# Four edits to a fused linear-attention and SwiGLU kernel: the order of its opening, the split of a weight block, the place of the row sums, and the last chunk of the output

## The chip, the cores and the metric

The kernel runs on one core of one Trainium2 chip. The metric is the device time of one execution in microseconds (us), of which several are taken; medians are quoted. Profiles show one execution each, and their span is 1.8 to 2.2 us shorter than the time of the same execution. Times in a profile count from the start of its span. All runs here were in the fast state (granted TensorE clock 0.995 to 1.0; 0.979 to 0.981 in the run with merged stores). "PE" is TensorE, "DVE" VectorE, "ACT" ScalarE, "POOL" GpSimd, "SP" the engine whose queue issues most transfers.

## The reference

```python
# attention: B=8, H=8, S=576, D=64          FFN: 4608 rows, d_model=512, d_ff=1536
kv  = einsum('bhsd,bhse->bhde', k, v)
out = einsum('bhsd,bhde->bhse', q, kv)
x   = out / sqrt(mean(out*out, -1) + 1e-6) * g_norm        # per head, then heads side by side
xn  = x / sqrt(mean(x*x, -1) + 1e-6) * rms_g
y   = (silu(xn @ w_gate) * (xn @ w_val)) @ w_out           # float32
```

## The kernel before

The rows are done in nine batches: the first 512 rows of each of the eight sequences, then their last 64 rows together. For each batch PE does twelve "up" units (the gate and the val products of 128 of the 1536 columns) and four "down" chunks. The attention of batch n+1 is woven between the up units of batch n. Weights arrive as float32, and are scaled and cast to bf16 ("rounded") on ACT, DVE or POOL.

The loads of the opening all go through one queue, in this order: k, v and q of batch 0, the weight blocks, k of batch 1, a third of w_out, v and q of batch 1, the rest of w_out, batch 2. The weight blocks, and what batch 0 does with the third one (units 4 to 7):

```python
W_BLOCKS = [(0, 2), (2, 4), (4, 8), (8, 12)]          # in units of 128 columns

def load_w(blk, name, queue):
    j0, j1 = W_BLOCKS[blk]
    ...                                               # a staging tile, [128, NS, columns]
    queue.dma_start(out=ap, in_={"g": wg_view, "v": wv_view}[name][:, :, j0 * 128 : j1 * 128])
...
for s in range(2):
    round_w(2, "g", s, SC)                            # SC is ACT
    round_w(2, "v", s, DVE)
for i in range(2):
    ffn.gate_pair(i, 256, ffn.up_pair(i, 256))        # units 0..3, second half of the rows
    round_w(2, "g", 2 + i, SC)
    round_w(2, "v", 2 + i, DVE)
```

The first two units take their 512 rows in halves of 256 (A, then Z), whose attention runs just before. PE is kept busy by dummy products (`warm`) while it waits. The state of batch 0 goes out of PSUM in two copies of 64x64 for each pair of heads:

```python
def put_state0(j, ps):
    for u in range(2):
        rows = slice(u * D, u * D + D)
        DVE.tensor_copy(out=kv_all[rows, 0, j, rows], in_=ps[rows, rows])
```

At the end of batch 0, with the q of batch 1 cast by three instructions on DVE and one on ACT:

```python
for i in range(4):
    cast_q(1, slice(2 * i, 2 * i + 2), SC if i == 2 else DVE)
...
down_part(0, 0, 4); down_part(1, 0, 4)
att1.kv_products((0, 1, 2, 3)); att1.kv_copy()
down_part(2, 0, 4)
turns.q_turn(0, SC); turns.q_turn(1, DVE)             # PE turns q of batch 1
down_part(3, 0, 4)
round_wo(1, 0, 2, DVE)                                # second third of w_out
```

In the later batches, the place of the attention's steps by unit (`o` is the product, `sums` the row sums on DVE, `head`, `guess` and `root` the norm, `scale` and `x_rows` the scaled x and its transpose by DMA, issued on the SP queue):

```python
kv0, os = (2, (4, 5, 7, 8)) if n == 1 else (0, (2, 4, 6, 8))
for c, u in enumerate(os):
    steps[u].append(lambda a=a, c=c: a.o(c))
    steps[u + 1].append(lambda a=a, c=c: a.sums(c))
steps[10] += [a.head]
steps[11] += [a.guess, a.root]
for c in range(T):
    steps[11] += [lambda a=a, c=c: a.scale(c), lambda a=a, c=c: a.x_rows(c)]
```

The last batch stores each chunk, after one copy of 128x512 on ACT, by two transfers on the SP queue.

## Time and profile before

| | before |
|---|---|
| time, median of the first 3 runs | 327.01 us |
| span of the profile | 325.2 us |
| PE busy | 315.5 us, 97% |
| first product of the FFN | 17.9 us |
| end of batch 0's up units | 40.7 us |
| first product of batch 1 | 56.94 us |
| last product ends, then span ends | 320.75, 325.2 us |

PE is the engine to look at, and since it is busy at 97% the only thing to gain is the time in which it waits or runs dummies. The page of the kernel before, its first part (busy us, share of the span, instructions):

```profile
PE 315.5 (97%) x1908; PEld 156.4 (48%) x1908; DVE 181.7 (56%) x374; ACT 178.3 (55%) x314; POOL 16.8 (5%) x37
```

PE's waits in the kernel before (who waited for whom: total us, times, longest):

```profile
PE g_ps L471 <- DMA xnt<-xna: 0.8, 1, 0.8
PE v_ps L471 <- DVE wv_sb L203: 0.6, 1, 0.6
```

The first of these two lines is one hole in the middle, before batch 3; PE's waits list has nothing else after 57 us. The second, like the lines left out here, is of the opening. Here is the hole in the timeline of the kernel before (start, length, engine, instruction, and in brackets the idle time before it and what ended it):

```profile
112.83 10.52 PE L508 MATMUL o_ps<-wo_sb,h_sb 128*128 128x512 bf16 x48
115.75 2.50 DVE L377 TENSOR_TENSOR xna<-outa,s1y 128x512 bf16<-128x512 bf16 x4
116.53 6.26 SPq L384 DMA_TRANSPOSE xnt<-xna  x4
124.17 1.02 PE L471 MATMUL g_ps<-xnt,wg_sb 128*128 128x512 bf16 x4 [0.81 <-DMA xnt<-xna]
```

DVE starts to scale x 2.92 us after the down chunks begin (115.75 - 112.83); four transposes follow on SP, and the last lands too late. From the start of this down phase to batch 3 it is 11.34 us, where the next batches take 10.36: the hole with its restart costs 0.98 us.

Why the last one is late, the DMA view of the stretch from 115 to 122 us shows. Beside the packets of the transposes it has one packet of a queue that the profile labels "instruction" (queue: packets, MB, share of 16 engines):

```profile
q8 instruction: 1, 0.02, 1.2%
```

In the trace this is one packet of 16 KB, under way from 117.18 to 118.47 us. The first transpose, which overlaps it, takes 2.34 us to issue and lands after 3.48; the other three take 1.21 to 1.22 us and land after about 2.5.

The opening is bound by loads. The stretches of the kernel before (columns: stretch, its length, busy time and count of PE, weight loads, DVE, ACT, POOL, then granted clock, DMA share, GB/s):

```profile
18.00:20.00 2.00, 1.95 (x20) 1.50 (x18) 1.77 (x7) 1.44 (x4) 1.72 (x4) 1.00 1.05 381
20.00:22.00 2.00, 2.00 (x25) 1.82 (x23) 2.00 (x6) 1.94 (x3) 1.83 (x4) 1.00 1.05 389
22.00:24.00 2.00, 2.00 (x21) 1.81 (x19) 1.12 (x2) 1.24 (x2) 0.15 (x1) 1.00 1.03 382
```

The DMA share is 1.03 to 1.05 here, so the engines are not idle; that a transfer then lands when the bytes ahead of it have gone through is the author's estimate from this. The q of batch 1 shows what the landing means for PE (timeline before):

```profile
42.63 0.62 ACT L106 CAST qb<-st 128x512 bf16<-128x512 f32 x1 [0.86 <-DMA st<-in_q_dram]
42.70 1.09 DVE L108 CAST qb<-st 128x512 bf16<-128x512 f32 x3
44.66 1.06 PE L780 MATMUL att_ps<-identity,qb 128*128 128x128 bf16 x16
45.35 1.17 POOL L108 CAST wo_sb<-st 128x512 bf16<-128x512 f32 x2 [6.12 <-DMA st<-in_moe_w_out_dram]
46.37 0.70 DVE L108 CAST wo_sb<-st 128x1024 bf16<-128x1024 f32 x1
```

It lands at 42.6, is cast by 43.8, and PE turns it at 44.66: slack of 0.9 us. And the tail before, the last copy and the two stores behind it (timeline of all engines, then SP alone):

```profile
320.79 0.59 ACT L106 COPY o_sb<-o_ps 128x512 f32<-128x512 f32 x1 [2.00 <-PE o_ps L508]
```

```profile
321.40 1.11 SPq L521 DMA_DIRECT2D out_dram<-o_sb  x2
```

### The profile page before, as it was taken

To read this page: it belongs to the slowest core of one execution; us is meant where nothing else is said; L and a number is where in the kernel's file an instruction comes from. 1 tells how busy PE (TensorE), PEld (TensorE's weight loads), DVE (VectorE), ACT (ScalarE), POOL (GpSimd) and SP (SyncE) were. 2 spreads that over 40 slices of the span, in tenths; PEclk is the share of its full clock that TensorE was granted. 3 is DMA by queue.
4 is the path that set the end of the run, shared out by engine and by line. 5 is a ranking of instruction groups with operands and counts; after the bars stand their busy time and mean duration, and the time that the engine had idled before them with its cause. 6 is when DMAs were issued, how large, how long until landed. Compare 5 with 4: busy or idle time off the path is not lost.

```text
span 325.2 us, 5068 instructions
## 1 busy us (share of the span) xinstructions
PE 315.5 (97%) x1908; PEld 156.4 (48%) x1908; DVE 181.7 (56%) x374; ACT 178.3 (55%) x314; POOL 16.8 (5%) x37
## 2 busy tenths in 40 slices
PE   7899999999999998999999999999999999999994
PEld 3684455544454444444544454445544444444441
DVE  4876657569436852676167715780578057904310
ACT  3567357666756575557655755666554355233321
POOL 1251323000000000000000000000000000000000
PEclk9999999999999999999999999999999999999999
DMA  8999999794369626971696179956200640060014
GB/s 260 346 379 387 376 373 290 211 288 133 64 177 289 152 46 162 303 171 33 161 315 170 33 147 199 299 156 156 81 2 16 159 85 0 18 179 1 0 34 98
DMA packets 73861, 54.87 MB, mean 169 GB/s; under 512 B 42088, under 2 KB 65644, under 8 KB 73836
## 3 DMA queue, kind: packets, MB, share of 16 engines
q1 hardware_dynamic: 73536, 53.95, 59.1%
q10 hardware_dynamic: 300, 0.59, 0.5%
q8 instruction: 15, 0.25, 0.3%
q14 instruction: 10, 0.08, 0.1%
HBM read 37.75 MB, written 9.44 MB: 145 GB/s over the span
## 4 chain that ended last, share of the span: by engine, by line
PE 90%; DMA 5%; SPq 1%; DVE 1%; POOL 1%; issue 0%; ACT 0%
PE g_ps L471 28%; PE v_ps L471 27%; PE o_ps L508 26%; DMA st<-in_moe_w_val_dram 3%; PE att_ps L271 2%; DMA st<-in_q_dram 2%; PE att_ps L342 2%; PE v_ps L488 1%; SPq L384 1%; PE g_ps L508 1%; PE g_ps L488 1%; PE v_ps L508 1%; DMA xnt<-xna 1%; POOL wv_sb L203 1%; PE att_ps L337 0%; PE att_ps L284 0%
## 5 line engine op out<-in xcount | busy, mean ns | idle before, releaser
L477 DVE TENSOR_TENSOR h_sb<-silu,v_ps 128x512 bf16<-128x512 bf16 x104 | 71.2, 685 | 110.3 <-PE v_ps L471 81.4
L471 PE MATMUL v_ps<-xnt,wv_sb 128*128 128x512 bf16 x416 | 106.9, 379 | 0.8 <-DVE wv_sb L203 0.6
L471 PE MATMUL g_ps<-xnt,wg_sb 128*128 128x512 bf16 x416 | 106.8, 379 | 0.8 <-DMA xnt<-xna 0.8
L476 ACT ACTIVATE silu<-g_ps 128x512 bf16<-128x512 f32 x104 | 62.6, 602 | 67.1 <-PE g_ps L471 66.0
L508 PE MATMUL o_ps<-wo_sb,h_sb 128*128 128x512 bf16 x408 | 90.0, 379 | 0.0
L508 PEld LDWEIGHTS <-h_sb 128*128 128x128 bf16 x432 | 41.9, 98 | 49.3 <-issue 0.3
L471 PEld LDWEIGHTS <-wv_sb 128*128 128x128 bf16 x416 | 40.7, 98 | 50.3 <-DVE wv_sb L203 1.2
L471 PEld LDWEIGHTS <-wg_sb 128*128 128x128 bf16 x416 | 38.5, 98 | 41.2 <-issue 2.2
L106 ACT COPY o_sb<-o_ps 128x512 f32<-128x512 f32 x34 | 19.9, 587 | 39.3 <-PE o_ps L508 39.3
L360 DVE TENSOR_REDUCE ssq<-sq 128x16 f32<-128x1024 bf16 x28 | 34.2, 1220 | 1.0
L351 ACT ACTIVATE sq<-att_ps 128x512 bf16<-128x512 f32 x28 | 16.7, 597 | 14.0 <-PE att_ps L342 11.2
L106 ACT CAST vb<-st 128x512 bf16<-128x512 f32 (+2 forms) x35 | 20.1, 627 | 4.0 <-DMA st<-in_v_dram 3.9
L377 DVE TENSOR_TENSOR xna<-outa,s1y 128x512 bf16<-128x512 bf16 x28 | 17.5, 687 | 0.2
L353 ACT CAST outa<-att_ps 128x512 bf16<-128x512 f32 x28 | 16.2, 580 | 0.0
L106 ACT CAST qb<-st 128x1024 bf16<-128x1024 f32 (+1 forms) x15 | 14.2, 987 | 1.9 <-DMA st<-in_q_dram 1.9
L106 ACT CAST kb<-st 128x512 bf16<-128x512 f32 (+1 forms) x25 | 14.0, 619 | 0.0
L359 DVE TENSOR_TENSOR sq<-sq,gsq 128x512 bf16<-128x512 bf16 x28 | 11.7, 418 | 0.0
L342 PEld LDWEIGHTS <-qt 128*128 128x128 bf16 x96 | 7.4, 98 | 5.7
L342 PE MATMUL att_ps<-kv_all,qt 128*128 128x128 bf16 x96 | 9.3, 219 | 0.0
L271 PEld LDWEIGHTS <-kb 128*128 128x128 bf16 x120 | 7.7, 98 | 2.8
L583 PE MATMUL att_ps<-kv_all 128*128 128x256 bf16 (+1 forms) x34 | 7.6, 357 | 1.2 <-DVE sel L572 1.2
L271 PE MATMUL att_ps<-vb,kb 128*128 128x128 bf16 x120 | 8.7, 219 | 0.0
(123 smaller groups left out, 154.4 us busy)
## 6 DMA issues: line engine op xcount, KB each, us to landing
out_dram<-o_sb SPq DMA_DIRECT2D x16, 512.0 KB, 3.2
st<-in_q_dram SPq DMA_DIRECT2D x7, 1024.0 KB, 7.3
st<-in_k_dram SPq DMA_DIRECT2D x6, 1024.0 KB, 10.3
st<-in_v_dram SPq DMA_DIRECT2D x6, 1024.0 KB, 11.6
st<-in_moe_w_out_dram SPq DMA_DIRECT2D x3, 1024.0 KB, 13.4
st<-in_moe_w_gate_dram SPq DMA_DIRECT2D x2, 1024.0 KB, 12.3
st<-in_moe_w_val_dram SPq DMA_DIRECT2D x2, 1024.0 KB, 13.1
st<-in_k_dram SPq DMA_DIRECT2D x4, 288.0 KB, 4.9
```

The source lines that it names most:

```text
L106: engine.copy(out=dst, in_=src)
L271: PE.matmul(ps, lhsT=bufs[b]["k"][:, t, hs, :], rhs=bufs[b]["v"][:, t, hs, :], start=(first and t == 0), stop=(last and t == T),)
L342: PE.matmul(cols, lhsT=self.qt[:, j, 128 * c : 128 * c + 128], rhs=kv_all[:, self.n, j, :], start=(j == 0), stop=(j == NS - 1),)
L351: SC.activation(out=self.sq[c][:, 0], in_=ps, func=ACT.Square)
L353: SC.copy(out=self.outa[c], in_=ps)
L359: DVE.tensor_tensor(out=sq[:, 1], in0=sq[:, 0], in1=gsq8, op=OP.mult)
L360: DVE.reduce_sum(out=self.ssq[:, c], in_=sq, axis=AX.X)
L377: DVE.tensor_tensor(out=self.xna[c], in0=self.outa[c], in1=self.alpha[:, c, :].to_broadcast([128, H, D]), op=OP.mult)
L471: PE.matmul(ps, lhsT=wt[:, s, j * 128 : (j + 1) * 128], rhs=x[:, s, :], start=(s == 0), stop=(s == NS - 1),)
L476: SC.activation(out=silu, in_=g_ps, func=ACT.Silu)
L477: DVE.tensor_tensor(out=self.h[:, j, :], in0=silu, in1=v_ps, op=OP.mult)
L508: PE.matmul(self.o_ps[c], lhsT=self.h[:, j, c * 128 : (c + 1) * 128], rhs=wo_sb[:, j, :], start=(j == 0), stop=(j == NF - 1),)
```

## The change

Four edits in one. (1) The opening is reordered: one state copy of 128x128, casts of q moved off DVE's critical stretch (one to POOL), the first gate products in quarters, so that they can start after one turned chunk of x. (2) The third weight block is split in two, so that units 4 and 5 have their weights sooner, and POOL rounds half of each. (3) The sums, the head and the guess move up one unit. (4) The last chunk is computed in three column parts, copied by ACT, ACT and DVE, and stored in halves on two queues. The core of the diff:

```diff
-    W_BLOCKS = [(0, 2), (2, 4), (4, 8), (8, 12)]
+    W_BLOCKS = [(0, 2), (2, 4), (4, 6), (6, 8), (8, 12)]
...
     def put_state0(j, ps):
-        for u in range(2):
-            rows = slice(u * D, u * D + D)
-            DVE.tensor_copy(out=kv_all[rows, 0, j, rows], in_=ps[rows, rows])
+        DVE.tensor_copy(out=kv_all[:, 0, j, :], in_=ps[:, 0:128])
...
+    ffn = Ffn(0)
+    first = ffn.pair_banks()
+    for lo in (0, 128):
+        for u in range(2):
+            ffn.half_unit(first[0], u, wg_sb, u, lo, lo + 128)
     oZ = rows_of(Z)
+    for u in range(2):
+        ffn.half_unit(first[1], u, wv_sb, u, 0, 256)
...
-    for s in range(2):
-        round_w(2, "g", s, SC)
-        round_w(2, "v", s, DVE)
+    for s in range(NS):
+        round_w(2, "g", s, SC if s < 2 else GP)
+        round_w(2, "v", s, DVE if s < 2 else GP)
     for i in range(2):
-        ffn.gate_pair(i, 256, ffn.up_pair(i, 256))
-        round_w(2, "g", 2 + i, SC)
-        round_w(2, "v", 2 + i, DVE)
+        banks = [b.rearrange("p (u t) -> p u t", u=2) for b in rows_banks()] if i == 0 else None
+        ffn.gate_pair(i, 256, ffn.up_pair(i, 256, banks=banks))
     broadcast_gsq()
+    for s in range(NS):
+        round_w(3, "g", s, SC if s < 2 else GP)
+        round_w(3, "v", s, DVE if s < 2 else GP)
...
-            kv0, os = (2, (4, 5, 7, 8)) if n == 1 else (0, (2, 4, 6, 8))
+            kv0, os = (2, (4, 5, 7, 8)) if n == 1 else (0, (2, 4, 6, 7))
-            steps[10] += [a.head]
-            steps[11] += [a.guess, a.root]
+            late = int(n == 1)
+            steps[9 + late] += [a.head]
+            steps[10 + late] += [a.guess]
+            steps[11] += [a.root]
...
+        def down_last(self, c):
+            o_sb = osb_pool.tile([128, 2, d_model], FP32, name="o_sb")[:, 0, :]
+            parts = (
+                (0, 256, ops_pool, "o_ps", SC), (256, 384, gps_pool, "g_ps", SC), (384, 512, vps_pool, "v_ps", DVE),
+            )
+            for lo, hi, p, nm, engine in parts:
+                ...                                  # 12 products of hi - lo columns
+                cast(engine, o_sb[:, lo:hi], ps)
+                for d0, done in ((0, 256), (256, 512)):
+                    if hi == done:
+                        for u in range(2):
+                            r0 = (2 * c + u) * S + MAIN
+                            (nc.sync if u or hi < d_model else nc.scalar).dma_start(
+                                out=out[r0 : r0 + TAIL, d0:done], in_=o_sb[u * TAIL : (u + 1) * TAIL, d0:done]
+                            )
```

(Also in the diff: fewer and longer dummy products, the order of the casts and of the gate scale, the rounding of the fourth block under its new number.)

More of the change, by code (lines that the diff above doesn't have):

```diff
@@ L477, in up, with pair_banks, half_unit, up_pair @@
             DVE.tensor_tensor(out=self.h[:, j, :], in0=silu, in1=v_ps, op=OP.mult)
-        def up_pair(self, i, lo, between=()):
-            x = xnts[self.n]
-            g_ps = gps_pool.tile([128, 2, 256], FP32, name="g_ps")
-            v_ps = vps_pool.tile([128, 2, 256], FP32, name="v_ps")
-            for ps, wt in ((g_ps, wg_sb), (v_ps, wv_sb)):
-                for u in range(2):
-                    j = 2 * i + u
-                    for s in range(NS):
-                        PE.matmul(
-                            ps[:, u, :], lhsT=wt[:, s, j * 128 : (j + 1) * 128], rhs=x[:, s, lo : lo + 256],
-                            start=(s == 0), stop=(s == NS - 1),
-                        )
-                    for f in between[2 * (wt is wv_sb) + u :][:1]:
+        def pair_banks(self):
+            return (
+                gps_pool.tile([128, 2, 256], FP32, name="g_ps"),
+                vps_pool.tile([128, 2, 256], FP32, name="v_ps"),
+            )
+        def half_unit(self, ps, u, wt, j, lo, hi):
+            for s in range(NS):
+                PE.matmul(
+                    ps[:, u, lo % 256 : lo % 256 + hi - lo], lhsT=wt[:, s, j * 128 : (j + 1) * 128],
+                    rhs=xnts[self.n][:, s, lo:hi], start=(s == 0), stop=(s == NS - 1),
+                )
+        def up_pair(self, i, lo, between=(), banks=None):
+            banks = banks or self.pair_banks()
+            for k, wt in enumerate((wg_sb, wv_sb)):
+                for u in range(2):
+                    self.half_unit(banks[k], u, wt, 2 * i + u, lo, lo + 256)
+                    for f in between[2 * k + u :][:1]:
                         f()
-            return g_ps, v_ps
+            return banks
         def gate_pair(self, i, lo, banks):
@@ L534, in down @@
             self.down_out(c)
+        def down_last(self, c):
+            o_sb = osb_pool.tile([128, 2, d_model], FP32, name="o_sb")[:, 0, :]
+            parts = (
+                (0, 256, ops_pool, "o_ps", SC), (256, 384, gps_pool, "g_ps", SC), (384, 512, vps_pool, "v_ps", DVE),
+            )
+            for lo, hi, p, nm, engine in parts:
+                ps = p.tile([128, MAIN], FP32, name=nm)[:, 0 : hi - lo]
+                for j in range(NF):
+                    PE.matmul(
+                        ps, lhsT=self.h[:, j, c * 128 : (c + 1) * 128], rhs=wo_sb[:, j, lo:hi],
+                        start=(j == 0), stop=(j == NF - 1),
+                    )
+                cast(engine, o_sb[:, lo:hi], ps)
[5 more added lines that the diff above has]
+                                out=out[r0 : r0 + TAIL, d0:done], in_=o_sb[u * TAIL : (u + 1) * TAIL, d0:done]
+                            )
     DVE.memset(kv_all[:, B - 1], 0.0)
@@ L599, in turn_q0 @@
         bank = att_pool.tile([128, 512], FP32, name="att_ps")
-        warm(bank, dummies, 256)
+        warm(bank, dummies)
         ps = bank.bitcast(BF16).rearrange("p (j i t) -> p j i t", j=NS, i=2)
@@ L615, in state0 @@
         ps = att_pool.tile([128, 512], FP32, name="att_ps")
-        warm(ps, dummies, 256)
+        warm(ps, max(dummies, 1), 512 if dummies else 128)
         kv_pair(ps[:, 0:128], 0, j, True, True)
@@ L641, in x_turn, with rows_banks @@
         to_rows(x, cols.n, cols.lo // 128 + c, bank.bitcast(BF16)[:, 0:512].rearrange("p (j t) -> p j t", j=NS), engine)
+    def rows_banks():
+        return [ops_pool.tile([128, MAIN], FP32, name="o_ps") for _ in range(2)]
     def rows_of(cols):
-        banks = [ops_pool.tile([128, H, D], FP32, name="o_ps") for _ in range(2)]
+        banks = [b.rearrange("p (h d) -> p h d", h=H) for b in rows_banks()]
         for c in range(2):
@@ L657 @@
     kv0 = state0(0, 0)
-    kv1 = state0(1, 5)
+    kv1 = state0(1, 3)
     put_state0(0, kv0)
@@ L662 @@
     put_state0(1, kv1)
-    qps = turn_q0(0, 4)
+    qps = turn_q0(0, 2)
     cast_kv(0, "k", 2, DVE)
@@ L667 @@
     put_q0(0, qps, 1, SC)
-    kv2 = state0(2, 6)
-    cast_kv(0, "k", 3, DVE)
-    cast_kv(0, "v", 3, SC)
-    put_state0(2, kv2)
-    gam_ps = att_pool.tile([128, 8], FP32, name="att_ps")
+    gam_ps = att_pool.tile([128, 512], FP32, name="att_ps")
     PE.matmul(gam_ps[:, 0:5], lhsT=gam[0:5, :], rhs=ident32[0:5, 0:5], is_transpose=True, start=True, stop=True)
@@ L675 @@
     DVE.tensor_scalar(out=rowscale, in0=gam_ps[:, 0:NS], scalar1=gcol[:, 0:1], scalar2=None, op0=OP.mult)
-    DVE.scalar_tensor_tensor(
-        out=gsq, in0=gcol, scalar=1.0 / d_model, in1=gcol, op0=OP.mult, op1=OP.mult
-    )
-    for i in range(2):
-        DVE.tensor_copy(out=sel[i * D : (i + 1) * D, 1, i : i + 1], in_=gsq[i * D : (i + 1) * D, :])
+    kv2 = state0(2, 3)
+    cast_kv(0, "k", 3, DVE)
+    put_state0(2, kv2)
+    cast_kv(0, "v", 3, DVE)
     banksA = [gps_pool.tile([128, MAIN], FP32, name="g_ps"), vps_pool.tile([128, MAIN], FP32, name="v_ps")]
@@ L686 @@
     square(A, 2, banksA[1])
-    kv3 = state0(3, 2)
+    kv3 = state0(3, 1)
+    DVE.scalar_tensor_tensor(
+        out=gsq, in0=gcol, scalar=1.0 / d_model, in1=gcol, op0=OP.mult, op1=OP.mult
+    )
     put_state0(3, kv3)
-    cast_q0(1, hs0, DVE)
-    cast_q0(1, hs1, DVE)
+    for i in range(2):
+        DVE.tensor_copy(out=sel[i * D : (i + 1) * D, 1, i : i + 1], in_=gsq[i * D : (i + 1) * D, :])
     A.alloc_sums()
-    warm(A.bank, 4, 256)
+    warm(A.bank, 1)
     columns(A, 3, banksA[1])
     square(A, 3, banksA[1])
-    warm(A.bank, 3, 256)
+    warm(A.bank, 1)
     A.sums()
     oA = rows_of(A)
+    cast_q0(1, hs0, DVE)
+    cast_q0(1, hs1, GP)
+    A.head()
     qps = turn_q0(1, 0)
-    A.head()
     A.root_by_table(lambda: put_q0(1, qps, 0, DVE))
@@ L703 @@
         for s in range(NS):
-            round_w(0, name, s, GP)
+            if name == "g" or s < 2:
+                round_w(0, name, s, GP)
     banksZ = [gps_pool.tile([128, MAIN], FP32, name="g_ps"), vps_pool.tile([128, MAIN], FP32, name="v_ps")]
-    warm(banksZ[0], 4, 256)
+    warm(banksZ[0], 2)
     for j in range(NS):
@@ L710 @@
     squares(Z, 1, banksZ[1])
+    for s in (2, 3):
+        round_w(0, "v", s, SC)
     xs = [A.scale(c, oA[c]) for c in range(2)]
-    x_turn(A, 0, xs[0], DVE, 1)
+    x_turn(A, 0, xs[0], DVE)
     x_turn(A, 1, xs[1], DVE)
@@ L722 @@
     SC.preload_act_table(ACT.Silu)
-    ffn = Ffn(0)
     xs = [Z.scale(c, oZ[c]) for c in range(2)]
@@ L728 @@
     clear_tail_rows(0, GP)
-    halves = [ffn.up_pair(0, 0)]
     def turnsZ():
@@ L733, in turnsZ @@
         x_turn(Z, 1, xs[1], DVE)
-    halves.append(ffn.up_pair(1, 0, (lambda: None, turnsZ)))
-    ffn.gate_pair(0, 0, halves[0])
-    ffn.gate_pair(1, 0, halves[1])
-    for blk in (2, 3):
+    second = ffn.up_pair(1, 0, (lambda: None, turnsZ))
+    ffn.gate_pair(0, 0, first)
+    ffn.gate_pair(1, 0, second)
+    for blk in (2, 3, 4):
         for name in ("g", "v"):
@@ L756, in broadcast_gsq @@
         DVE.tensor_copy(out=gsq8, in_=ps[:, 0:D].unsqueeze(1).to_broadcast([128, H, D]))
-    for s in range(2):
-        round_w(2, "g", s, SC)
-        round_w(2, "v", s, DVE)
+    for s in range(NS):
+        round_w(2, "g", s, SC if s < 2 else GP)
+        round_w(2, "v", s, DVE if s < 2 else GP)
     for i in range(2):
-        ffn.gate_pair(i, 256, ffn.up_pair(i, 256))
-        round_w(2, "g", 2 + i, SC)
-        round_w(2, "v", 2 + i, DVE)
+        banks = [b.rearrange("p (u t) -> p u t", u=2) for b in rows_banks()] if i == 0 else None
+        ffn.gate_pair(i, 256, ffn.up_pair(i, 256, banks=banks))
     broadcast_gsq()
+    for s in range(NS):
+        round_w(3, "g", s, SC if s < 2 else GP)
+        round_w(3, "v", s, DVE if s < 2 else GP)
     alloc_q(1)
@@ L789 @@
     for s in (2, 3):
-        round_w(3, "v", s, GP)
+        round_w(4, "v", s, GP)
     for j in range(4, NF):
@@ L793 @@
         for s in {4: (0, 1), 5: (2,), 6: (3,)}.get(j, ()):
-            round_w(3, "g", s, SC)
+            round_w(4, "g", s, SC)
         if j == 6:
             for s in (0, 1):
-                round_w(3, "v", s, DVE)
+                round_w(4, "v", s, DVE)
         if j >= 8:
@@ L951 @@
                 ffn.up(unit)
+            elif n == B and unit == NF + T - 1:
+                ffn.down_last(unit - NF)
             else:
```

## The prediction

> **What bounds the kernel now.** TensorE. The page has PE busy 315.5 of 325.2 us at full clock. Three places are open. (1) The opening: the stretches view shows PE busy 2.91, 3.09, 3.67, 3.83 of 4 us from 4 to 20 us, partly dummy matmuls; the first FFN product starts at 17.9; batch 0's up phase ends at 40.7, though 12 units of 1.73 need 20.8. (2) A hole of 0.81 us at 123.3, before batch 3, on the DMA transpose of x; PE waits nowhere else after 57 us. (3) The tail: last matmul ends at 320.8, copy of 512 columns 0.59, two stores issued one after the other (321.4, 321.9), end 325.2.
>
> **The opening is also bound by loads.** The DMA rows show 345 to 390 GB/s from 4 to 52 us, and casts wait for landings: second block's val weights 25.4, third 31.0, output weights 36.6, q of batch 1 about 42.6, output weights 45.35 and 48.1. The change moves no byte ahead of batch 1's q, so these times should stay.
>
> **Opening.** State copies: two of 0.23 become one of about 0.25, four times. The q casts leave DVE's way; quarters let PE start after one turned chunk; v rounding is shared with ACT. First FFN product: 17.9 to about 16.8. The second pair's val weights still land about 20.1, so units 2-3 gain only 0.4. The split block removes most waits of units 4 and 5: the up phase ends about 39.2, 1.5 us early. Then batch 1's q at 42.6 plus three DVE casts (1.09) holds PE's q turn to about 43.8, against 44.66 before. **Of 1.5 us only about 0.85 survives**; the rest becomes a new PE wait of 0.5 to 1.3 us near 43.
>
> **Sums.** Before batch 3, DVE does unit 11's product, guess 0.9 and root 0.68, then scales from 115.75. Sums, head and guess move up a unit, but four units then carry 8.0 us of DVE work in about 7.1, so a backlog eats part: scales 0.65 earlier, hole 0.81 to 0.2. Gain 0.6.
>
> **Tail.** 128-column matmuls run at about 0.055 us each in the trace, so 12x256 + 24x128 cost as much as 12x512 (2.6). The last copy falls from 0.59 to about 0.28, and the last two stores start together on two queues, saving one issue (0.55). [...] Gain 0.85.
>
> **Sum:** 0.85 + 0.6 + 0.85 = 2.3: 327.0 to **324.7 us**, range 323.3 to 326.2 for 8 in 10. Faster by over 2%: 0.02; within 2%: 0.96; slower by over 2%: 0.02.
>
> **What would show it.** PE's waits: a new one on the DVE q cast of batch 1, the wv_sb wait gone; batch 1's first product near 56.1 (before 56.94); the wait before batch 3 below 0.4; other batches still 33.1 apart; the last copy on DVE near 0.28 and the end 3.3 to 3.6 us after the last matmul instead of 4.4.
>
> **What would make it wrong.** Loads landing at other times (earlier: up to 0.7 more is kept); POOL's rounding of half of the split blocks late against PE; DVE's backlog holding a PSUM bank, with new PE waits at units 9 to 11 in every batch; 128-column matmuls slower than thought.

## The result, and the profile after

The changed kernel took 325.53 us (325.46 to 325.61, 4 runs), the kernel before 326.68 us (326.2 to 327.15, 4 runs). The ratio is 0.9965, 95% interval 0.9947 to 0.9983. The gain is 1.15 us; 2.3 were predicted.

| us, from the profiles | before | after |
|---|---|---|
| first product of the FFN | 17.90 | 17.62 |
| end of batch 0's up units | 40.71 | 39.59 |
| q of batch 1 has landed | 42.63 | 43.22 |
| first product of batch 1 | 56.94 | 57.01 |
| start of batch 2's down chunks, to batch 3 | 11.34 | 10.36 |
| last product's end, to the end of the span | 4.47 | 3.88 |
| span | 325.2 | 323.6 |

So the whole gain of the opening, 1.1 us at the end of the up units, is gone before batch 1 begins. From PE's waits in the changed kernel:

```profile
PE att_ps L633 <- DVE qb L108: 1.1, 1, 1.1
...
PE o_ps L515 <- DVE wo_sb L108: 0.3, 1, 0.3
```

The wait on the turned x is not in the list any more. (The first line is at 8.7 us, for the q of batch 0. The wait for the q of batch 1 falls on the weight loads of the turn, so that it is not in this list, but the timeline shows it.) What holds PE at the end of batch 0 (timeline after):

```profile
43.22 1.10 DVE L108 CAST qb<-st 128x512 bf16<-128x512 f32 x3 [1.56 <-DMA st<-in_q_dram]
43.22 0.62 ACT L106 CAST qb<-st 128x512 bf16<-128x512 f32 x1 [1.74 <-DMA st<-in_q_dram]
43.70 0.10 PEld L820 LDWEIGHTS <-qb 128*128 128x128 bf16 x1 [0.49 <-DVE qb L108]
43.71 1.74 PE L820 MATMUL att_ps<-identity,qb 128*128 128x128 bf16 x16
...
45.97 1.63 POOL L108 CAST wo_sb<-st 128x512 bf16<-128x512 f32 x2 [6.14 <-DMA st<-in_moe_w_out_dram]
46.09 1.04 DVE L108 CAST wo_sb<-st 128x1024 bf16<-128x1024 f32 x1
```

The turn of q takes 1.74 us instead of 1.06, because it starts while the casts still run. The late turn leaves 0.28 of the 1.1 us: the products behind it start at 45.28, in the kernel before at 45.56. The wait for the cast of w_out then takes what is left: the products behind that start at 47.18, in the kernel before at 47.12. The wait for q was predicted. But the landing was not: q comes 0.6 us later than before, at 43.22, and so does w_out, at 45.97 instead of 45.35. The stretches of the changed kernel say where the 0.6 us arose:

```profile
18.00:20.00 2.00, 2.00 (x30) 1.90 (x28) 1.79 (x8) 1.28 (x4) 0.64 (x1) 1.00 1.10 350
20.00:22.00 2.00, 2.00 (x24) 1.78 (x23) 2.00 (x6) 1.99 (x4) 1.75 (x4) 1.00 1.10 348
22.00:24.00 2.00, 2.00 (x20) 1.77 (x19) 1.98 (x4) 1.50 (x4) 1.54 (x4) 1.00 1.10 352
```

The DMA engines are as busy as before (share 1.10 against 1.03 to 1.05), yet move 350 GB/s instead of 384. Over 6 us that is 0.20 MB less (34 GB/s x 6 us), or 0.53 us at 384 GB/s. This is the time in which the split block is loaded: 256 columns of float32 are rows of 1 KB, where the whole block has rows of 2 KB. The packets in the traces have these sizes: from 20 to 22 us the kernel before has 380 of 2 KB, which take 88 ns each on average, and the changed kernel 680 of 1 KB, which take 51 ns.

The hole before batch 3 (timeline after): DVE starts to scale 1.90 us after the down chunks begin, 1.02 earlier than before, and PE goes from batch to batch without a wait.

```profile
112.85 10.52 PE L515 MATMUL o_ps<-wo_sb,h_sb 128*128 128x512 bf16 x47
114.75 2.50 DVE L377 TENSOR_TENSOR xna<-outa,s1y 128x512 bf16<-128x512 bf16 x4
115.50 5.19 SPq L384 DMA_TRANSPOSE xnt<-xna  x4
123.21 1.03 PE L471 MATMUL g_ps<-xnt,wg_sb 128*128 128x512 bf16 x4
```

The four transposes also took 5.19 us on SP, not 6.26, and the DMA view of their stretch has no instruction packet; an experiment comes back to that. The tail (all engines, then SP alone):

```profile
318.93 0.83 PE L552 MATMUL v_ps<-wo_sb,h_sb 128*128 128x128 bf16 x12
319.85 0.29 DVE L108 COPY o_sb<-v_ps 128x128 f32<-128x128 f32 x1 [9.72 <-PE v_ps L552]
320.23 0.56 ACTq L561 DMA_DIRECT2D out_dram<-o_sb  x1
```

```profile
320.46 0.54 SPq L561 DMA_DIRECT2D out_dram<-o_sb  x1
```

The copy is as short as predicted, 0.29 us, and ends at 320.14. The ACT queue starts its store 0.09 us later, the SP queue only 0.32 us later.

### The profile page after: what moved, and what is told of

The parts are those of the page before. It is cut to its first block, busy times and chain, and to the rows that moved or that the text cites. A ratio compares the mean times of both kernels' runs of the same rounds, so it can differ in the third digit from the quotient of the medians.

```text
span 323.6 us, 5091 instructions
## 1 busy us (share of the span) xinstructions
PE 313.3 (97%) x1891; PEld 156.5 (48%) x1925; DVE 180.9 (56%) x371; ACT 177.3 (55%) x316; POOL 21.5 (7%) x44
## 2 busy tenths in 40 slices
DMA packets 75077, 54.87 MB, mean 170 GB/s; under 512 B 42152, under 2 KB 68012, under 8 KB 75052
## 4 chain that ended last, share of the span: by engine, by line
PE 81%; DMA 10%; DVE 3%; SPq 3%; issue 1%; POOL 0%; ACT 0%; DVEq 0%
PE o_ps L515 25%; PE g_ps L471 24%; PE v_ps L471 24%; DMA st<-in_q_dram 7%; DMA st<-in_moe_w_val_dram 3%; SPq L193 2%; PE att_ps L271 2%; PE att_ps L342 2%; DVE h_sb L477 1%; PE v_ps L515 1%; PE g_ps L515 1%; PE att_ps L337 0%; PE o_ps L552 0%; DVE ssq L360 0%; DVE qb L108 0%
## 5 line engine op out<-in xcount | busy, mean ns | idle before, releaser
L471 PE MATMUL g_ps<-xnt,wg_sb 128*128 128x512 bf16 x403 | 105.1, 379 | 0.8 <-ACT wg_sb L201 0.2
L471 PE MATMUL v_ps<-xnt,wv_sb 128*128 128x512 bf16 x407 | 105.5, 379 | 0.4
L515 PE MATMUL o_ps<-wo_sb,h_sb 128*128 128x512 bf16 x387 | 87.0, 379 | 0.8 <-DVE wo_sb L108 0.3
L515 PEld LDWEIGHTS <-h_sb 128*128 128x128 bf16 x420 | 40.7, 98 | 48.3 <-issue 0.6
L106 ACT COPY o_sb<-o_ps 128x512 f32<-128x512 f32 (+1 forms) x34 | 19.7, 579 | 38.1 <-PE o_ps L515 36.3
L612 PE MATMUL att_ps<-kv_all 128*128 128x512 bf16 (+1 forms) x19 | 6.9, 497 | 1.9 <-DVE sel L601 1.2
```

Source lines behind the costliest of these rows:

```text
L106: engine.copy(out=dst, in_=src)
L471: PE.matmul(ps, lhsT=wt[:, s, j * 128 : (j + 1) * 128], rhs=x[:, s, :], start=(s == 0), stop=(s == NS - 1),)
L515: PE.matmul(self.o_ps[c], lhsT=self.h[:, j, c * 128 : (c + 1) * 128], rhs=wo_sb[:, j, :], start=(j == 0), stop=(j == NF - 1),)
```

## The experiments

Kernels are compared only within the same rounds. All outputs are right.

### One part of the change at a time

**Sums alone:** the kernel before with only the edit of `os`, `head`, `guess` and `root` shown above.

> The kernel before with only the sums, head and guess moved up one unit. Theory: this part alone closes the hole before batch 3 and is worth 0.8 to 1.0 us (0.997 to 0.9975 of before); the PE wait on the turned x disappears and everything before it stays where it was. Rival: the hole in the changed kernel closed because of the opening's shift of the loads, and then this run shows the hole of about 0.8 us still there and no gain.

Measured: 325.91 us against 326.97, ratio 0.9962 (0.9945 to 0.998). In its profile, batch 3 starts 10.36 us after batch 2's down chunks, without a wait, and batch 1 starts at 57.04. The theory holds: the opening is as before and the hole is closed. This one edit is worth as much as the whole change. From the timeline:

```profile
115.59 5.96 SPq L384 DMA_TRANSPOSE xnt<-xna  x4
...
123.28 1.03 PE L471 MATMUL g_ps<-xnt,wg_sb 128*128 128x512 bf16 x4
```

The instruction packet is still there, at 117.47 us: the first transpose lands after 4.09 us and the second takes 2.01 to issue. So what keeps PE from waiting in this run is the earlier start, not a faster transpose.

**Last chunk alone:** the kernel before with `down_last`.

> The kernel before with only the last chunk in column parts. Theory: worth 0.5 to 0.6 us, with the end about 3.85 us after the last matmul instead of 4.4, because the last SP store starts only when the store ahead of it has been issued. Rival (as predicted): 0.85 us, end 3.5 us after.

Measured: 326.81 us against 326.97, ratio 0.999 (0.9973 to 1.0008): no gain is shown. The profile has 4.12 us from the last product to the end, instead of 4.47. All eight profiles with such a tail (but for the merged stores below) have 3.78 to 4.12 us there, the five with the old one 4.47 to 4.54, so it is worth 0.35 to 0.75 us in the traces. Neither number of the expectation is met well, and the timing alone is too coarse to decide between them. The hole before batch 3 is in this profile too, but smaller (timeline):

```profile
116.71 5.89 SPq L384 DMA_TRANSPOSE xnt<-xna  x4
...
123.97 1.02 PE L471 MATMUL g_ps<-xnt,wg_sb 128*128 128x512 bf16 x4 [0.44 <-DMA xnt<-xna]
```

**Opening and split alone:** the changed kernel with the sums and the last chunk as before.

> The changed kernel with the sums and the last chunk as before: only the opening and the split weight block. Theory: worth nothing, 0.0 plus or minus 0.2 us; the up phase of batch 0 ends 1.1 us earlier, but q of batch 1 lands about 0.6 us later (43.2 instead of 42.6) and batch 1 starts at 57.0 as before. Rival: the late landing in the changed kernel's trace was chance; then q lands at 42.6, batch 1 starts near 56.1 and the run gains 0.8 us.

Measured: 326.44 us against 326.97, ratio 0.998 (0.9961 to 0.9999), which is more than the theory's 0.2 us and less than the rival's 0.8. In the profile, the load rate from 18 to 24 us is 349 to 352 GB/s again, q of batch 1 lands at 42.94, and batch 1 starts at 56.79 (before: 56.94). This profile has no hole before batch 3, though its sums are as before:

```profile
112.64 10.52 PE L515 MATMUL o_ps<-wo_sb,h_sb 128*128 128x512 bf16 x47
115.57 2.50 DVE L377 TENSOR_TENSOR xna<-outa,s1y 128x512 bf16<-128x512 bf16 x4
116.33 5.17 SPq L384 DMA_TRANSPOSE xnt<-xna  x4
123.00 1.03 PE L471 MATMUL g_ps<-xnt,wg_sb 128*128 128x512 bf16 x4
```

DVE starts to scale 2.93 us after the down chunks, as in the kernel before (2.92), and yet there is no wait. The difference is the issue of the transposes: 5.17 us here, 6.26 before.

The 14 profiles together show what it goes with. They hold 392 of these transposes. Nineteen took over 1.3 us to issue, and each of the nineteen overlaps a 16 KB packet of the instruction queue; the 364 that overlap none took 1.25 us at most. All six profiles with the old opening have such a packet among the transposes before batch 3 (at 116.9 to 117.9 us): there the first lands after 3.3 to 4.1 us, and the first or the second takes up to 2.34 us to issue. None of the eight with the new opening has one there (in the changed kernel it comes at 124.0 us, in this run at 125.1). The profiles divide in this way, so the late landing is no accident of one execution: it goes with the opening. That the opening does it by moving later instruction packets in time is argued from these traces; no run was made for it.

So the rival of the run with the sums alone holds as well: in the traces either edit alone closes the hole, the sums by an earlier start, the opening because no packet falls there. In the changed kernel both apply, and the 0.98 us can't be given to one of them. It can't be counted twice either: alone, the three parts gain 1.06, 0.16 and 0.53 us by the medians, 1.75 in sum; together they gain 1.15.

With the old place of the sums the schedule has about 0.2 us to spare (an estimate from this profile: the last transpose is issued at about 120.3, takes some 2.45 us to land, and PE needs it at 123.0). Of the four profiles with that place and the packet, three have a hole (waits of 0.8, 0.7 and 0.2 us in all). With the new place, 1.02 us earlier, the schedule has about 1.2 by the same estimate, and none of the nine profiles with the sums moved shows a hole, though two of them have the packet.

### The packets of the split block

Two kernels test the 1 KB rows by themselves. Both are the kernel before, with each load of the third weight block issued as two halves into the same staging tile:

```diff
+        view = {"g": wg_view, "v": wv_view}[name][:, :, j0 * 128 : j1 * 128]
+        for h in range(2 if blk == 2 else 0):
+            cut = (slice(None), slice(None), slice(256 * h, 256 * h + 256))    # columns: rows of 1 KB
+            # the other kernel: (slice(None), slice(2 * h, 2 * h + 2), slice(None)), rows of 2 KB
+            queue.dma_start(out=ap[cut], in_=view[cut])
```

> The kernel before, with each of the two loads of the third weight block issued as two halves by columns (rows of 1 KB) into the same tile, nothing else. Theory (small packets): the rate from 18 to 24 us falls from 381 to 389 to about 350 GB/s, the third block's val weights are complete about 0.55 us later, q of batch 1 lands near 43.2, and batch 1 starts 0.4 to 0.6 us later (time 0.3 to 0.6 us above before). Rival (more, smaller transfers cost; the packets don't): the other run of this pair shows the same loss.

> The same as its pair, with the halves cut by rows instead (two of the four row groups each, packets of 2 KB): as many transfers, of the same size, but large packets. Theory (small packets): rate from 18 to 24 us as before, 381 to 389 GB/s, q of batch 1 at 42.6, time as before within 0.2 us. Rival (number of transfers): 350 GB/s and the same loss as its pair.

Measured, on the same chip: columns 327.22 us, rows 326.78, before 326.94; ratios to before 1.0018 (1.0005 to 1.003) and 0.999 (0.9978 to 1.0002). The rate, in the stretch from 20 to 22 us, and the landing of q, first of the halves by columns, then by rows (a fence for each view):

```profile
20.00:22.00 2.00, 2.00 (x23) 1.60 (x22) 2.00 (x5) 1.97 (x4) 1.72 (x4) 1.00 1.10 349
```

```profile
43.32 0.62 ACT L106 CAST qb<-st 128x512 bf16<-128x512 f32 x1 [0.79 <-DMA st<-in_q_dram]
```

```profile
20.00:22.00 2.00, 2.00 (x25) 1.83 (x23) 2.00 (x6) 1.99 (x3) 1.68 (x4) 1.00 1.04 386
```

```profile
42.74 0.62 ACT L106 CAST qb<-st 128x512 bf16<-128x512 f32 x1 [1.74 <-DMA st<-in_q_dram]
```

As many transfers of the same size move 349 GB/s with rows of 1 KB and 386 with rows of 2 KB; q lands 0.58 us apart. So it is the packets, not the number of transfers. The page's DMA part agrees: 65,644 packets under 2 KB before, 67,724 with the columns cut, 65,676 with the rows cut, 68,012 in the changed kernel. The DMA share is 1.10 with the columns cut and 1.04 with the rows cut, so the engines were idle in neither, and the split with rows of 1 KB lost 10% of the rate.

The halves by rows gained something that was not expected: batch 1 starts at 56.52, since the first two row groups can be rounded before the second half has landed. The time (326.78) does not settle whether that lasts.

### The block whole again, rounded by three engines

If the packets cost 0.6 us and the gain of units 4 and 5 comes from POOL's help with the rounding, the split can go. The changed kernel with:

```diff
-    W_BLOCKS = [(0, 2), (2, 4), (4, 6), (6, 8), (8, 12)]
+    W_BLOCKS = [(0, 2), (2, 4), (4, 8), (8, 12)]
...
     for s in range(NS):
         round_w(2, "g", s, SC if s < 2 else GP)
-        round_w(2, "v", s, DVE if s < 2 else GP)
+    for s in (2, 3):
+        round_w(2, "v", s, GP)
     for i in range(2):
         ...
         ffn.gate_pair(i, 256, ffn.up_pair(i, 256, banks=banks))
+        if i == 0:
+            for s in (0, 1):
+                round_w(2, "v", s, DVE)
     broadcast_gsq()
-    for s in range(NS):
-        round_w(3, "g", s, SC if s < 2 else GP)
-        round_w(3, "v", s, DVE if s < 2 else GP)
```

> The changed kernel with the third weight block loaded whole again (rows of 2 KB instead of 1 KB), but rounded by ACT, POOL and DVE together. Theory (small packets): the rate from 18 to 24 us is back at 381 to 389 GB/s instead of 348 to 352, all later loads land about 0.6 us earlier (q of batch 1 at 42.6, output weights at 45.4), the up phase still ends near 39.6 and batch 1 starts 0.4 to 0.6 us earlier than in the changed kernel: about 325.0 us. Rival (the split is needed so that PE doesn't wait in units 4 and 5, and the packets cost nothing): q still lands at 43.2, or PE waits more in units 4 and 5 than it saves, and the time is 325.5 us or more.

Measured: 325.25 us against 326.97, ratio 0.9949 (0.9928 to 0.997). Both ran again side by side:

> The changed kernel once more, as a measure beside the other three on the same chip: 325.5 us, ratio to before about 0.996.

> The changed kernel with the third block loaded whole and rounded by three engines, once more, on the same chip as the changed kernel. Theory: 0.3 to 0.6 us faster than the changed kernel, batch 1 starting 0.5 us earlier. Rival: the two are the same within 0.15 us, and the earlier advantage was the difference between two sets of runs.

Measured: changed kernel 325.83 us (325.54 to 326.21), whole block 325.04 us (324.96 to 325.19), before 327.00. The ratio of the two means is 325.08 / 325.86 = 0.9976, and no run of the one reaches the range of the other. Ratios to before: 0.9963 (0.9945 to 0.9981) and 0.9939 (0.9922 to 0.9956). The profile of the second run with the whole block has the rate and the landings back (the middle stretch of the three, which are at 381, 385 and 389 GB/s, then the timeline):

```profile
20.00:22.00 2.00, 2.00 (x24) 1.70 (x23) 2.00 (x6) 1.99 (x3) 1.94 (x4) 1.00 1.04 385
```

```profile
42.53 0.62 ACT L106 CAST qb<-st 128x512 bf16<-128x512 f32 x1 [1.55 <-DMA st<-in_q_dram]
...
43.87 1.06 PE L821 MATMUL att_ps<-identity,qb 128*128 128x128 bf16 x16
```

The up units end at 39.92 (40.20 in the changed kernel), so nothing was lost there, and batch 1 starts at 56.31 instead of 57.09. This kernel beats both.

### Is the reordered opening needed?

The kernel before with its own opening, the block whole and rounded by three engines as in the last diff, and the sums and last chunk as changed:

> The kernel before with its own opening (two state copies, casts, no quarters) and the whole third block, but that block rounded by ACT, POOL and DVE together; sums and last chunk as changed. Theory (the start of the opening is bound by the second block's load, which lands at about 20.1 us, so its reordering gives nothing): up phase ends near 39.6 to 39.8, batch 1 starts within 0.2 us of the run with the changed opening, the time is the same within 0.2 us. Rival (the reordering is worth its 0.3 us of earlier start): batch 1 starts 0.3 us or more later.

Measured: 325.31 us (324.75 to 325.55); with the reordered opening 325.04. Batch 1 starts at 56.73 instead of 56.31. By the profile the rival is right, by the time the difference of 0.27 us lies within the spread of the runs. The reordering may be worth 0.4 us or nothing: this is left open. What the traces do show is where the 1.1 us at the end of the up units come from. The second pair's val products start at 21.20 us in the kernel before and at 21.15 in the changed kernel, and PE does not wait there in either. Unit 5 then begins at 28.63 and at 27.51: nearly all of the gain is in unit 4, where the kernel before waits for rounded val weights (the 0.6 us in its list of waits). With the old opening and the shared rounding, in this run, unit 4 goes without a wait too (26.70 to 28.43). So sharing the rounding is enough for that part.

The first product's step from 17.90 to 17.62 is not a sign of more: eight attention products, 0.44 us, now stand behind the first gate products instead of before them. Over all the profiles the first product lies at 17.9 to 18.4 us with the old opening and at 17.2 to 17.9 with the new.

### Two attempts at what is left

**One of the q casts to POOL** (whole block, and `cast_q(1, ..., (DVE, DVE, SC, GP)[i])`):

> The changed kernel with the whole third block, and one of the three q casts of batch 1 that DVE does given to POOL. Theory: after the landing PE still waits for the casts (1.1 us on DVE); with two on DVE and one each on ACT and POOL they end about 0.3 us sooner, and batch 1 starts up to 0.3 us earlier than with the whole block alone, unless the output weights' landing at 45.4 takes it back. Rival: only the landings count, no change.

Measured: 325.32 us, ratio to before 0.9959 (0.9947 to 0.9971); batch 1 starts at 56.56. No gain. The timeline tells why (DVE, then POOL):

```profile
42.79 1.18 DVE L108 CAST qb<-st 128x512 bf16<-128x512 f32 x2 [0.81 <-DMA st<-in_q_dram]
```

```profile
42.82 0.87 POOL L108 CAST qb<-st 128x512 bf16<-128x512 f32 x1 [3.44 <-DMA st<-in_q_dram]
```

Two casts on DVE beside one on POOL take 1.18 us, where three on DVE alone take 1.10. In the opening of the changed kernel, where POOL's cast of q begins first, POOL's takes 0.61 and DVE's beside it 0.70, where DVE's first cast of that size, alone, took 0.43. So a cast of 128x512 on DVE takes longer while one runs on POOL: 0.59 us here (1.18 for two), 0.37 with none there (1.10 for three). And POOL's takes 0.87 here, 0.61 where it begins first. What makes them slower was not shown. The same shows in the changed kernel's profile above: the cast of w_out on DVE takes 1.04 us beside POOL's, and took 0.70 before, when it came later and met POOL's for only 0.15 us.

**The two stores of each chunk of the last batch merged into one** (on top of that, `rows = out.rearrange("(b s) d -> b s d", s=S)[2 * c : 2 * c + 2, MAIN:S, :]` as the target of all 128 partitions):

> The same with the two stores of each chunk of the last batch merged into one (128 partitions, one transfer), all on the SP queue. Theory (the last store waits for the issue of the ones before it): with four stores fewer, the last store is issued right after the last copy, and the end comes about 3.5 us after the last matmul instead of 3.84: 0.3 us less. Rival: the time from issue to landing counts, and a store of twice the size takes as much longer: no gain.

Measured: 338.86 us, ratio 1.0365 (1.0352 to 1.0379): slower by 12 us, all in the tail. The last chunk's copies wait for earlier stores (timeline), and the stretch shows why they are late:

```profile
325.56 0.37 ACT L106 COPY o_sb<-o_ps 128x256 f32<-128x256 f32 x1 [8.12 <-DMA out_dram<-o_sb]
```

```profile
320.00:322.00 2.00, 0.00 (x0) 0.00 (x0) 0.00 (x0) 0.00 (x0) 0.00 (x0) 1.00 0.13 51
```

The stores move 51 GB/s, with a DMA share of 0.13, as much as two of 16 engines busy all the time (0.13 x 16 = 2.1, an estimate). The stores of the kernel before, 64 rows each, move 207 GB/s at a share of 0.91 (320 to 321 us). The target of a merged store has the pair of sequences, of size 2, as its outermost dimension; whether that is the reason was not tried. Two stores of 64 rows each are the faster form here, and the experiment says nothing about the theory that it was made for.

That theory got a test of its own, with the whole block and the second store of the last chunk's first half on the ACT queue, so that the SP queue is free:

```diff
-    (nc.sync if u or hi < d_model else nc.scalar).dma_start(
+    (nc.sync if u == (hi == d_model) else nc.scalar).dma_start(
```

> The changed kernel with the whole third block, and the second store of the last chunk's first half moved from the SP queue to the ACT queue. Theory (the last SP store waits for the issue of the one ahead of it, 320.45 instead of 320.2): the end comes 0.2 to 0.3 us sooner after the last matmul, 3.55 to 3.65 us instead of 3.84. Rival: the landing of the last store decides, no change.

Measured: 325.53 us, ratio to before 0.9956 (0.9938 to 0.9973), and the end 3.88 us after the last product, against 3.78 without this edit. The theory falls. The last copy and store (all engines, then SP alone):

```profile
319.42 0.29 DVE L108 COPY o_sb<-v_ps 128x128 f32<-128x128 f32 x1 [9.72 <-DMA out_dram<-o_sb]
319.80 0.47 ACTq L561 DMA_DIRECT2D out_dram<-o_sb  x1
```

```profile
320.12 0.47 SPq L561 DMA_DIRECT2D out_dram<-o_sb  x1
```

SP had ended the issue before at 319.07 (318.53 + 0.54), and still started only 0.41 us after the copy's end at 319.71, the ACT queue after 0.09. So it is not the issue ahead that holds the SP store. In the built program this store waits for three semaphores (an earlier transfer, DVE, ACT), the one on the ACT queue for two, and the changed kernel's trace has the same waits (SP at 320.40 and 320.46 us, ACT at 320.17 and 320.23); whether that is the reason was not tried.

## Why the prediction was right or wrong

The time, 325.53 us, lies in the range and "within 2%" was right. But the gain was half of what was predicted, and the sum of 0.85 + 0.6 + 0.85 was made of terms that were each off. That the time lies in the range is in part luck: the hole gave 0.4 us more than predicted, and the opening 0.9 less.

- **Opening, 0.85 predicted.** In the traces it is -0.07 to -0.15 in the changed kernel (batch 1 at 57.01 and 57.09, before 56.94); timed alone it is 0.53 with an interval of 0.03 to 1.3 us, but that run's profile has lost the hole too, so this is no measure of the opening by itself. The step that failed: "The change moves no byte ahead of batch 1's q, so these times should stay." The bytes stayed, the packets did not: rows of 1 KB went at 350 instead of 384 GB/s, and q and w_out landed 0.6 us later. The list of what would make the prediction wrong had "loads landing at other times", but gave a size only to earlier landings. The mechanism around it was right: the up units end early (39.6; 39.2 was predicted), PE waits for q, and the turn of q is bound by the landing plus the casts. The first product of the FFN moved by 0.3 us instead of 1.1, and in this pair of profiles only by a change of order.
- **Sums, 0.6 predicted.** The hole's 0.98 us went, in the traces; the sums alone gain 1.06 by the medians. The mechanism was right, in that the earlier scales close the hole; the backlog on DVE was put too high. The scales come 1.02 us earlier against the down chunks (1.90 after them instead of 2.92), not 0.65. What the prediction did not see is why the hole was there: an instruction packet among the transposes, which the new opening moves away by itself. So this term and the opening's were not independent, as the sum took them to be.
- **Tail, 0.85 predicted.** 0.59 in these two traces (4.47 to 3.88), and 0.16 by the medians of the run alone, which has an interval that includes nothing and 0.85. The copy (0.28 predicted, 0.29 measured) and the speed of the narrow products (0.055 us each predicted; 12 of 128 columns in 0.67 us, 0.056 each) were right. Smaller stores do land a little sooner: in the changed kernel after 2.0 us for 64 KB and 2.4 for 128 KB (medians, from the issue). The term that was too large is the store: it was to start with the copy's end on both queues, and on SP it starts 0.32 us after it. The first explanation of that, the issue ahead of it, fell in an experiment; the cause stays open.
- The spans of the two profiles differ by 1.6 us and the times by 1.15. The profile before holds the longest hole that any profile here shows, so part of the difference may be that execution's.

## What to carry to other kernels

Where a stretch is bound by loads, measure what a finer split of a load costs. Here it was not free even at equal bytes: 349 GB/s with rows of 1 KB, 386 with rows of 2 KB. Look at the packet size that the split leaves, and at the GB/s in a stretch with the DMA share beside it; here a full share (1.10) with a lower rate meant smaller packets. If the aim of a split is an earlier start, first share the work behind the landing among engines, or split along rows that stay long. When a wait on a transfer appears in some kernels and not in others, look in the DMA view for instruction packets beside it (here, before batch 3, a transpose beside one of 16 KB landed after up to 4.1 us, one without after about 2.5), and compare all the profiles that there are before calling it chance. When two edits can close the same hole, don't add their gains: time each alone and both together.
